# A fused attention and feed-forward kernel: the fold of a pair's exponentials moves to GpSimd, and later input loads are issued by ScalarE

## The chip, the core and the metric

The kernel runs on one core of a Trainium2 chip. The metric is the device time of one execution in microseconds. Engines are named as in the profile: PE is TensorE (PEld its weight loads), DVE is VectorE, ACT is ScalarE, POOL is GpSimd, SP is SyncE. A queue name with q (SPq, ACTq) stands for DMA issues and semaphore waits of that engine's instruction stream.

## The reference

Two stages in fp32. Attention has 4 batches, 8 heads, 768 positions and head size 64; a query sees the 96 positions up to its own, and the first 8 positions of the sequence. Its result, reshaped to 3072 x 512, goes through a two-layer network of width 2048.

```
scores = scale * (q @ k^T);  keep = is_global | is_local
scores = where(keep, scores - slope[h] * dist, -1e9)
a = exp(scores - max); a = a / (sum(a) + 1e-9)
attn_out = a @ v
h = x @ w_in;  g = h * sigmoid(h);  out = g @ w_out
```

## The kernel before

**Tiling.** The sequence of each batch is cut into 6 blocks of 128 queries, 24 blocks in all (i = 0 to 23, j = i mod 6). A block has four pairs of heads. For one pair the scores are 232 columns: 96 keys of the preceding block, 8 global keys, 128 own keys. Two blocks make a group of 256 rows for the network, 12 groups in all. fp32 values are split into a high and a low fp32r part, and products are formed from three matmuls (high by high, high by low, low by high).

**One block of attention.** `load` (L513) fetches keys, queries and values of block i (tiles kn, qn, vn; line L520). `turn` (L557) transposes keys and queries on PE (L560). From block 6 on, ACT and DVE build split and stacked copies (L602, L600, L604, L619, L613). `stack_scores` (L628) forms the scores of one pair. On DVE `top_of` (L680) adds the bias and takes the maximum; on ACT `expo` (L688) takes the exponential with its sum; DVE forms the inverse (L695, L699); ACT scales (L708).

**The folded blocks.** The 15 blocks with i >= 7 and j > 0 are folded. Their 96 preceding keys are 96 of the 128 rows of the block before, and for each query a preceding key is seen only where the own key of the same row is not. So `fold` (L713 to L716) adds the 96 preceding exponentials onto the last 96 own ones, in place, in tile pe. `collect` (L721) copies the 8 global columns to FARS. `turn_folded` (L736, and L739 for the globals of two pairs) transposes the sum on PE, `part_p` (L744) separates it into the two parts by a mask, `move_far` (L751) brings in the globals, and `values` (L789) multiplies by vn and by vp, the preceding values. There are 60 pairs in folded blocks.

**The network.** `pair_h` (L1079) forms two 128-wide pieces of the hidden layer, 24 matmuls of 256 columns. ACT takes tanh (L1085), DVE forms the gate (L1091), POOL forms four sums and differences (L1097), ACT rounds to the high part gh (L1121), DVE forms the low part gl (L1127), and `pair_o` (L1156) multiplies by the second weights with 21 matmuls, some of them from tiles tx and ty, which are loaded from a scratch in HBM for every group (L1065, L1069). At a group's end DVE adds up the results (L1188), and L1024 stores them. Between these, DVE also reads the weights and the values for a range check (L473, L490).

**What sets the order.** `Plan` is a planner in the kernel's own Python code. Every operation is entered by `op(engine, cost, rank, emit, deps, uses, lat)`; `run` (L104) plays the machine forward with these costs and latencies, at each moment gives a free engine the ready operation of the lowest rank, and so fixes the order in which the instructions of each engine stand. SP's DMA issues are one more planner engine, "DMA". The engines then run their streams in that order and wait on semaphores. Buffers are counted there too: kn and qn take two of twelve slots of the shared tag m, vn has two slots.

**Places that the change touches.** The load itself, L520; the planner entries of the loads of k and q (L846) and of v (L879); `fold`, L716, and its planner entry, L923. The blocks from NJ + NB = 8 on are the ones whose loads of k and q wait in the plan for the preceding transposition (`before["t"]`).

Of the kernel before, what the change touches and what calls it, by code (L numbers as in the profile page):

```python
# [17 lines left out]
ALU = mybir.AluOpType  # L18
# [4 lines left out]
NPREV = 96  # L23
# [163 lines left out]
def attn_moe(ctx, tc, q, k, v, n_global, n_local, w_in, w_out, out):  # L187
    nc = tc.nc
# [4 lines left out]
    NJ = S // P  # L193
    NCC = DM // P
    NFC = DFF // P
    NB = 2
# [166 lines left out]
    op = plan.op  # L363
    FIRST = -1e6
    DVE = lambda n: 1000 * (62 + n) / 960
    ACT = lambda n, over=61: 1000 * (over + n) / 1200
# [86 lines left out]
    for n in range(2 * NFC):  # L453
        rank = PAR["C0"] + PAR["CR"] * n
        a, m, x = [] if lent(n) is not None else [Buf("big")], Buf("mid", "m"), lent(n)
        o = op("DMA", 1456, rank - PAR["LW"], (lambda n=n: stage(n, "w")), [o_l[x]] if not a else (), a, PAR["DW"])
# [56 lines left out]
    def load(i, nm, h0=0, h1=H):  # L513
        b, j = divmod(i, NJ)
        pool, tag = (sb2, "vn") if nm == "v" else (sb3, in_kind(i, nm))
        pool = mid if tag == "m" else pool
        if not h0:
            blk[i][nm] = pool.tile([P, H, D], F32, name=f"{nm}n", tag=tag, bufs=dict(vn=2, m=NM2, big=4)[tag])
        src = dict(k=k, q=q, v=v)[nm]
        nc.sync.dma_start(  # L520
            blk[i][nm][:, h0:h1], src[b, h0:h1, j * P:(j + 1) * P, :].rearrange("h p d -> p h d")
        )

# [189 lines left out]
    def fold(i, hp):  # L713
        x = blk[i]["p", hp]
        o = x[:, :, C1 + NGAP:]
        nc.vector.tensor_add(o, o, x[:, :, :NPREV])  # L716

    def collect(i, hp):
        t = blk[i]
# [106 lines left out]
    before, held, joint = {}, [], None  # L826
    for i in range(B * NJ):
# [15 lines left out]
        for nm in "kq" if i else "":  # L843
            xn, tp = Buf("big") if in_kind(i, nm) == "big" else Buf("qkn", "m"), Buf("tq")
            hi, lo = kk[nm.upper() + "H"], kk[nm.upper() + "L"]
            o = op("DMA", 1456, rank - lr if i < NJ + NB else FIRST + rank, (lambda i=i, nm=nm: load(i, nm)), () if i < NJ + NB else [before["t"]], [xn], PAR["DL" if i < NJ else "DX"])  # L846
            stacked = i >= PAR["I0"]
            own = [] if nm == "q" or not stacked or not j else [
                op("POOL", cost, rank, (lambda i=i, x=x, gl=gl: carry(i, x, gl)), [before["s"]], [kk["KH"], kk["KL"]])
# [21 lines left out]
        if j and i < PAR["I0"]:  # L871
            old = o_k[i - 1]
            for gl, cost in ((True, 270), (False, 540)):
# [2 lines left out]
                    [*(old[z] for z in ([("kh", *x) for x in PARTS] if i == 1 else ("kh",))), old.get(("KH", True)), ob["kh"]],  # L876
                    [kb[i - 1]["KH"], kk["KH"]],
                )
        o_v = [op("DMA", 1456, rank - lr + 1, (lambda i=i: load(i, "v")), (), [kk["vn"]], PAR["DL" if i < NJ else "DX"])]  # L879
        arrived = o_v[0]  # L880
        if j:
            o_v.append(op("DMA", 1456 if folded(i) else 750, rank - lr + 1, (lambda i=i: load_prev(i)), o_vg if folded(i) else before["v"],
# [5 lines left out]
        for hp in range(NHP):  # L888
# [31 lines left out]
            o = op("DVE", 72, u - PAR["RI"], (lambda i=i, hp=hp: inverse(i, hp)), [o], [pe])  # L920
            if folded(i):
                far = [op("ACT", 480, u - PAR["RN"], (lambda i=i, hp=hp, a=a: norm(i, hp, a)), [o], [pe]) for a in range(2)]
                o = [op("DVE", 360, u - PAR["RN"], (lambda i=i, hp=hp: fold(i, hp)), far, [pe])]  # L923
                fb = before["far"] if hp % 2 else Buf("far")
                before["far"] = fb
                o.append(op("POOL", 300, u - PAR["RN"], (lambda i=i, hp=hp: collect(i, hp)), far, [pe, fb]))
                deps = [*o, joint]
                if not hp % 2:
                    deps = [o[0], joint]
                    before["collect"] = o[-1]  # L930
                else:
                    deps.append(before["collect"])
                o = op("PE", 328 if hp % 2 else 219, u - PAR["RP"], (lambda i=i, hp=hp, tp=tp: turn_folded(i, hp, tp)), deps, [pe, tp, *([fb] if hp % 2 else [])])
                o_m.append(op("DVE", 690, u - PAR["RM"], (lambda i=i, hp=hp: part_p(i, hp)), [o, before.get("move"), o_keep], [tp, pt]))
                before["move"] = o_m[-1]
                if hp % 2:
                    o_m.append(op("ACT", 550, u - PAR["RM"], (lambda i=i, hp=hp: move_far(i, hp)), o_m[-2:], [tp, pt, pts[-1]]))
                pts.append(pt)
                continue
# [681 lines left out]
```

## Time and profile before

| | |
|---|---|
| median of 3 runs | 665.17 us (664.48 to 665.78) |
| the profiled execution | 665.22 us, its span 663.5 us |
| PE busy | 652.3 us, 98% of the span |
| DVE busy | 570.9 us, 86% |
| ACT busy | 463.1 us, 70% |
| POOL busy | 173.8 us, 26% |
| granted TensorE clock | 1.00 in every stretch read |
| DMA engines | 74.4% of the span by SP's queue, 212 GB/s of HBM traffic |

The span runs from the first instruction to the last; the execution's time is 1.7 us longer. A busy share is an average over stages. Matmuls overlap, so that a busy PE says only that no gap was seen between one matmul's modelled end and the next one's start; the pace of the matmuls shows in the distance of their starts, or in the length of a run of them in the chain of work that ended last.

### The profile page before, as it was taken

Reading aid. Unit: us, or ns where it says so; the run is one execution under the profiler, and the core shown is the slowest. Engines: PE = TensorE matmul, PEld = TensorE weight load, DVE = VectorE, ACT = ScalarE, POOL = GpSimd, SP = SyncE. Lnnn points to the kernel's source line nnn. Section 1 sums busy time; section 2 is a strip of 40 time slices with the busy share of each in tenths; the row PEclk is TensorE's granted clock in tenths of the full one; section 3 lists DMA queues with packets and bytes.
Section 4 is the critical chain, followed back from the end, with each engine's and each line's share of the span. In section 5 each row is a group of like instructions: output and inputs, shape, how many; then the busy total and the mean of one; then the engine's idle time right before and its main releaser. Section 6 shows DMA issues by size and latency. Waiting matters only on the chain.

```text
span 663.5 us, 15861 instructions
## 1 busy us (share of the span) xinstructions
PE 652.3 (98%) x5666; PEld 624.6 (94%) x5666; DVE 570.9 (86%) x1554; ACT 463.1 (70%) x1146; POOL 173.8 (26%) x403
## 2 busy tenths in 40 slices
PE   7999999999999999999999999999999999999997
PEld 5788999889999999999999999999999999999997
DVE  7999999988878889978888988997897987996745
ACT  6997544588677777865877877785677787683333
POOL 3100000000104424424333434243343342442331
PEclk9999999999999999999999999999999999999999
DMA  9998857576798699759679668668867776868742
GB/s 183 234 295 243 245 172 234 165 238 194 215 270 231 195 274 263 229 167 279 196 202 251 190 191 230 208 205 221 257 194 195 236 228 181 261 165 206 218 157 82
DMA packets 157437, 142.62 MB, mean 215 GB/s; under 512 B 100228, under 2 KB 128324, under 8 KB 157356
## 3 DMA queue, kind: packets, MB, share of 16 engines
q1 hardware_dynamic: 157352, 141.58, 74.4%
q8 instruction: 45, 0.74, 0.5%
q14 instruction: 36, 0.29, 0.1%
q10 hardware_dynamic: 4, 0.00, 0.0%
HBM read 121.42 MB, written 19.12 MB: 212 GB/s over the span
## 4 chain that ended last, share of the span: by engine, by line
PE 91%; DVE 5%; ACT 2%; DMA 1%; issue 1%; ACTq 0%; DVEq 0%
PE bank L1079 34%; PE bank L1156 29%; PE bank L976 6%; PE bank L1001 6%; PE bank L789 5%; PE bank L628 5%; PE bank L560 2%; PE bank L736 2%; PE bank L764 1%; DVE pe L680 1%; DVE pe L710 1%; ACT pe L688 1%; DMA ts<-raww 1%; PE bank L739 0%; PE bank L1434 0%
## 5 line engine op out<-in xcount | busy, mean ns | idle before, releaser
L1097 POOL TENSOR_TENSOR sg<-sg 128x128 f32<-128x128 f32 x279 | 131.4, 491 | 217.6 <-DVE sg L1091 165.1
L1079 PE MATMUL bank<-xh,WIH 128*128 128x256 f32 x640 | 182.9, 286 | 0.0
L1079 PE MATMUL bank<-xl,WIH 128*128 128x256 f32 x640 | 178.0, 278 | 0.0
L1079 PE MATMUL bank<-xh,WIL 128*128 128x256 f32 x640 | 177.9, 278 | 0.0
L1127 DVE TENSOR_TENSOR gl<-sg,gh 128x512 fp32r<-128x512 f32 (+1 forms) x152 | 99.1, 653 | 28.5 <-ACT gh L1121 23.8
L1079 PEld LDWEIGHTS bank<-xh,WIH 128*128 128x128 f32 x640 | 120.6, 188 | 1.7 <-issue 1.2
L1121 ACT CAST gh<-sg 128x512 fp32r<-128x512 f32 (+1 forms) x152 | 84.6, 567 | 53.9 <-PE bank L1156 37.0
L1079 PEld LDWEIGHTS bank<-xl,WIH 128*128 128x128 f32 x640 | 120.6, 188 | 0.7 <-DVE xl L810 0.3
L1079 PEld LDWEIGHTS bank<-xh,WIL 128*128 128x128 f32 x640 | 120.4, 188 | 0.0
L688 ACT ACTIVATE pe<-pe,NM 128x232 f32<-128x232 f32 (+1 forms) x192 | 90.0, 472 | 13.1 <-DVE NM L680 11.1
L1085 ACT ACTIVATE sg<-bank 128x512 f32<-128x512 f32 x80 | 47.7, 596 | 42.1 <-PE bank L1079 41.1
L680 DVE CUSTOM_DVE_ANT_0 pe<-bank,B 128x232 f32<-128x232 f32 (+1 forms) x192 | 66.5, 373 | 8.1 <-PE bank L628 7.1
L1156 PE MATMUL bank<-WOH,gh 128*128 128x256 f32 (+1 forms) x280 | 73.3, 292 | 0.0
L1156 PE MATMUL bank<-WOL,gh 128*128 128x256 f32 (+1 forms) x280 | 72.6, 290 | 0.0
L708 ACT ACTIVATE pe<-pe,sm 128x232 f32<-128x232 f32 x132 | 58.6, 482 | 14.4 <-DVE sm L699 13.8
L1091 DVE SCALAR_TENSOR_TENSOR sg<-sg,bank 128x512 f32<-128x512 f32 x80 | 54.7, 684 | 12.9 <-ACT sg L1085 12.2
L1156 PEld LDWEIGHTS bank<-WOH,gh 128*128 128x128 f32 x280 | 52.8, 188 | 0.9
L1156 PEld LDWEIGHTS bank<-WOL,gh 128*128 128x128 f32 x280 | 52.7, 188 | 0.9
L1156 PE MATMUL bank<-WOH,gl 128*128 128x256 f32 (+1 forms) x280 | 49.5, 292 | 0.0
L1156 PE MATMUL bank<-tx,gh 128*128 128x256 f32 x288 | 46.9, 281 | 0.0
L721 POOL COPY FARS<-pe 128x16 f32<-128x16 f32 x60 | 17.5, 298 | 110.7 <-ACT pe L708 108.3
L744 DVE TENSOR_TENSOR pt<-bank,KEEP 128x512 f32<-128x512 f32 x60 | 41.0, 686 | 6.2 <-PE bank L739 4.2
(177 smaller groups left out, 1622.1 us busy)
## 6 DMA issues: line engine op xcount, KB each, us to landing
tx<-ts SPq DMA_DIRECT2D x72, 512.0 KB, 4.3
ty<-ts SPq DMA_DIRECT2D x72, 256.0 KB, 4.6
c<-in_moe_w_in_dram SPq DMA_DIRECT2D x16, 512.0 KB, 5.2
c<-in_moe_w_out_dram SPq DMA_DIRECT2D x16, 512.0 KB, 5.0
vn<-in_v_dram SPq DMA_DIRECT2D x24, 256.0 KB, 5.1
w<-in_moe_w_in_dram SPq DMA_DIRECT2D x12, 512.0 KB, 4.9
w<-in_moe_w_out_dram SPq DMA_DIRECT2D x12, 512.0 KB, 4.8
kn<-in_k_dram SPq DMA_DIRECT2D x23, 256.0 KB, 4.5
```

What stands on the lines that cost most here:

```text
L680: nc.vector.tensor_tensor_reduce(t["p", hp][:, a, :n], t["s", hp][a][:, :n], B1[:, hp] if i % NJ else B0[:, hp], -SC / (1 + a), 3.0e38, AL ...
L688: nc.scalar.activation(x, x, AF.Exp, bias=max_of(i, h), scale=-1.0, accum_out=t["sum", hp][:, a:a + 1],)
L708: nc.scalar.mul(x, x, t["inv", hp][:, a:a + 1])
L744: nc.vector.tensor_tensor(x, t["tp", hp].unsqueeze(1).to_broadcast([P, 2, 2, P]), KEEP.unsqueeze(2).to_broadcast([P, 2, 2, P]), ALU.mult)
L976: nc.tensor.matmul(ph, w[:, c, fs], x[:, c], start=not c and not n, stop=c == NCC - 1 and n == 2)
L1079: nc.tensor.matmul(ph[:, a], w[:, cc, fs], x[:, cc], start=not cc and not m, stop=cc == NCC - 1 and m == 2)
L1085: nc.scalar.activation(x[:, 0:4].rearrange("p (a b) c -> p a (b c)", a=2), mo["ph", g, n], AF.Tanh, scale=0.5)
L1091: nc.vector.scalar_tensor_tensor(x, x, 1.0, mo["ph", g, n], ALU.add, ALU.mult)
L1097: (eng.tensor_sub if e else eng.tensor_add)(x[:, o], x[:, a], x[:, b])
L1121: nc.scalar.copy(mo["gh", g, n][:, a:b], mo["sg", g, n][:, a + o:b + o])
L1127: nc.vector.tensor_sub(mo["gl", g, n][:, a:b], mo["sg", g, n][:, a + o:b + o], mo["gh", g, n][:, a:b].bitcast(F32))
L1156: nc.tensor.matmul(o, l, r, start=(g, b) not in opened, stop=n == NFC // 2 - 1 and m == 2 and (p in ((2, 7, 5, 3, 4) if g == NGRP - 1 else ...
```

## The change

1. `fold` is done by GpSimd (`nc.gpsimd.tensor_tensor(..., ALU.add)`) and not by VectorE. Its planner entry is ("POOL", 600) in place of ("DVE", 360).
2. The loads of keys, queries and values of blocks 8 to 23, 16 blocks with 3 loads each, are issued by ScalarE (`nc.scalar.dma_start`) and not by SyncE. Their planner entries take ACT for 420 in place of the DMA issue engine for 1456, and their latency is raised by 1000. The load of v now has a dependence on the preceding transposition too.

```diff
-        nc.sync.dma_start(
+        (nc.scalar if i >= NJ + NB else nc.sync).dma_start(
             blk[i][nm][:, h0:h1], src[b, h0:h1, j * P:(j + 1) * P, :].rearrange("h p d -> p h d")
         )
...
         o = x[:, :, C1 + NGAP:]
-        nc.vector.tensor_add(o, o, x[:, :, :NPREV])
+        nc.gpsimd.tensor_tensor(o, o, x[:, :, :NPREV], ALU.add)
...
-            o = op("DMA", 1456, rank - lr if i < NJ + NB else FIRST + rank, (lambda i=i, nm=nm: load(i, nm)), () if i < NJ + NB else [before["t"]], [xn], PAR["DL" if i < NJ else "DX"])
+            o = op(*(("DMA", 1456) if i < NJ + NB else ("ACT", 420)), rank - lr if i < NJ + NB else FIRST + rank, (lambda i=i, nm=nm: load(i, nm)), () if i < NJ + NB else [before["t"]], [xn], PAR["DL"] if i < NJ else PAR["DX"] + 1000 * (i >= NJ + NB))
...
-        o_v = [op("DMA", 1456, rank - lr + 1, (lambda i=i: load(i, "v")), (), [kk["vn"]], PAR["DL" if i < NJ else "DX"])]
+        o_v = [op(*(("DMA", 1456) if i < NJ + NB else ("ACT", 420)), rank - lr + 1, (lambda i=i: load(i, "v")), () if i < NJ + NB else [before["t"]], [kk["vn"]], PAR["DL"] if i < NJ else PAR["DX"] + 1000 * (i >= NJ + NB))]
...
-                o = [op("DVE", 360, u - PAR["RN"], (lambda i=i, hp=hp: fold(i, hp)), far, [pe])]
+                o = [op("POOL", 600, u - PAR["RN"], (lambda i=i, hp=hp: fold(i, hp)), far, [pe])]
```

Since the planner's costs change, the order moves on every engine from the ninth block on; the number of matmuls does not change. Three places follow, before and after.

VectorE at the end of the seventh group of the network, order before (ost is the group's result, few the range check's tile, sm the sums of one pair):

```order
L1091 SCALAR_TENSOR_TENSOR sg<-sg,bank_113 128x512
L744 TENSOR_TENSOR pt<-bank_115,KEEP 128x512
L695 TENSOR_SCALAR sm<-sm 128x2
L490 TENSOR_REDUCE few<-vn 128x1
L1188 SCALAR_TENSOR_TENSOR ost<-bank_119,ost 128x256
L1188 SCALAR_TENSOR_TENSOR ost<-bank_114,ost 128x256 x3
L1188 SCALAR_TENSOR_TENSOR ost<-bank_117,ost 128x256 x2
L1188 SCALAR_TENSOR_TENSOR ost<-bank_120,ost 128x256
L1127 TENSOR_TENSOR gl<-sg,gh 128x384
L699 RECIPROCAL sm<-sm 128x2
L613 SCALAR_TENSOR_TENSOR KH<-bank_116,KH 64x4x128
L1127 TENSOR_TENSOR gl<-sg,gh 128x512
```

The same place on VectorE, order of the change:

```order
L1091 SCALAR_TENSOR_TENSOR sg<-sg,bank_114 128x512
L744 TENSOR_TENSOR pt<-bank_117,KEEP 128x512
L1188 SCALAR_TENSOR_TENSOR ost<-bank_119,ost 128x256
L1188 SCALAR_TENSOR_TENSOR ost<-bank_120,ost 128x256 x3
L1188 SCALAR_TENSOR_TENSOR ost<-bank_113,ost 128x256 x2
L1188 SCALAR_TENSOR_TENSOR ost<-bank_115,ost 128x256
L1127 TENSOR_TENSOR gl<-sg,gh 128x384
L695 TENSOR_SCALAR sm<-sm 128x2
L613 SCALAR_TENSOR_TENSOR KH<-bank_118,KH 64x4x128
L1127 TENSOR_TENSOR gl<-sg,gh 128x512
```

Between the gate (L1091) and the second low part (the last row) the range check L490 and one of the two small steps on sm are gone and stand elsewhere. At the tenth group's end, which has the same rows before, the check stays where it was and only the step on sm goes.

GpSimd in the twelfth block, order before:

```order
L1097 TENSOR_TENSOR sg<-sg 128x128 x8
L721 COPY FARS<-pe 128x16 x3
L1097 TENSOR_TENSOR sg<-sg 128x128 x4
L721 COPY FARS<-pe 128x16
L1097 TENSOR_TENSOR sg<-sg 128x128 x12
```

The same block on GpSimd, order of the change:

```order
L1097 TENSOR_TENSOR sg<-sg 128x128 x8
L716 TENSOR_TENSOR pe<-pe 128x2x96
L721 COPY FARS<-pe 128x16
L716 TENSOR_TENSOR pe<-pe 128x2x96
L721 COPY FARS<-pe 128x16
L716 TENSOR_TENSOR pe<-pe 128x2x96
L1097 TENSOR_TENSOR sg<-sg 128x128 x4
L721 COPY FARS<-pe 128x16
L1097 TENSOR_TENSOR sg<-sg 128x128 x4
L716 TENSOR_TENSOR pe<-pe 128x2x96
L721 COPY FARS<-pe 128x16
L1097 TENSOR_TENSOR sg<-sg 128x128 x8
```

Every fold now stands in GpSimd's stream among the network's sums: 32 of the 60 come directly behind a set of them, and a set can stand between a fold and its collect.

ScalarE in the third batch, around the loads of block 13 (queries and values) and block 14 (keys), order before:

```order
L688 ACTIVATE pe,sm<-pe,NM 128x128
L1121 CAST gh<-sg 128x384
L602 CAST KH<-bank_114 64x4x128
L602 CAST KL<-bank_114 64x4x128
L1121 CAST gh<-sg 128x512
L1085 ACTIVATE sg<-bank_116 128x512
L1121 CAST gh<-sg 128x384
L602 CAST QH<-bank_119 64x512
L1121 CAST gh<-sg 128x512
L600 ACTIVATE QL<-bank_119 64x512
```

The same place on ScalarE, order of the change:

```order
L688 ACTIVATE pe,sm<-pe,NM 128x128
L1121 CAST gh<-sg 128x384
L520 DMA qn<-in_q_dram 128x8x64
L602 CAST KH<-bank_119 64x4x128
L1121 CAST gh<-sg 128x512
L602 CAST KL<-bank_119 64x4x128
L1085 ACTIVATE sg<-bank_118 128x512
L1121 CAST gh<-sg 128x384
L520 DMA kn<-in_k_dram 128x8x64
L1121 CAST gh<-sg 128x512
L520 DMA vn<-in_v_dram 128x8x64
L602 CAST QH<-bank_117 64x512
```

The three issues of a block stand between casts of the network's high parts and casts of the stacked keys and queries; the load of queries stands just ahead of the casts of the keys that were transposed before it.

## Rows read from the trace of the kernel before

**Rows 1.** Page, part 1: busy us, share of the span, instructions.

```profile
PE 652.3 (98%) x5666; PEld 624.6 (94%) x5666; DVE 570.9 (86%) x1554; ACT 463.1 (70%) x1146; POOL 173.8 (26%) x403
```

**Rows 2.** Stretches: length, busy PE, PEld, DVE, ACT, POOL; clock, DMA, GB/s.

```profile
200.00:250.00 50.00, 50.00 (x456) 49.09 (x455) 44.37 (x109) 38.35 (x93) 19.87 (x43) 1.00 0.76 228
...
640.00:663.50 23.50, 19.72 (x174) 19.52 (x173) 13.23 (x28) 7.20 (x14) 4.47 (x8) 1.00 0.21 65
```

**Rows 3.** Waits of PE, then of PEld, 160 to 600 us: total, times, longest.

```profile
PE bank L1156 <- DVE gl L1127: 0.6, 2, 0.3
...
PEld bank L1156 <- DVE gl L1127: 1.0, 2, 0.5
```

**Rows 4.** Timeline of PE, 417 to 418.5 us.

```profile
417.90 0.28 PE L1156 MATMUL bank<-WOH,gl 128*128 128x256 f32 x1
418.47 0.38 PE L1156 MATMUL bank<-tx,gl 128*128 128x256 f32 x1 [0.29 <-DVE gl L1127]
```

**Rows 5.** Chain that ended last: start, length; runs of 24 matmuls of 256 columns.

```profile
203.16 2.83 PE bank L1079 x24
...
611.11 2.72 PE bank L1079 x24
```

**Rows 6.** Timeline of DVE, 410 to 419 us: start, length, what.

```profile
413.12 0.67 DVE L490 TENSOR_REDUCE few<-vn 128x1 f32<-128x512 f32 x1
413.71 2.73 DVE L1188 SCALAR_TENSOR_TENSOR ost<-bank,ost 128x256 f32<-128x256 f32 x7
...
417.01 0.68 DVE L613 SCALAR_TENSOR_TENSOR KH<-bank,KH 64x512 fp32r<-64x512 f32 x1
417.72 0.69 DVE L1127 TENSOR_TENSOR gl<-sg,gh 128x512 fp32r<-128x512 f32 x1
```

**Rows 7.** Line L716, the fold: ns min/median/max, first and last start.

```profile
L716 DVE TENSOR_TENSOR pe<-pe x60: 341/358/639, 164.3 to 600.3; 128x192 f32<-128x192 f32 x60
```

**Rows 8.** Adds of two SBUF tiles: line L1097, then POOL's groups.

```profile
L1097 POOL TENSOR_TENSOR sg<-sg x279: 449/462/843, 201.3 to 654.1; 128x128 f32<-128x128 f32 x140
L1097 DVE TENSOR_TENSOR sg<-sg x9: 291/293/552, 646.2 to 655.4; 128x128 f32<-128x128 f32 x9
...
L1193 POOL TENSOR_TENSOR ost<-ost 128x256 f32<-128x256 f32 x1 | 0.7, 737 | 3.9 <-ACT ost L1185 3.9
```

**Rows 9.** Two folds and the transpositions that read them: timelines of DVE and PE.

```profile
418.93 0.35 DVE L716 TENSOR_TENSOR pe<-pe 128x192 f32<-128x192 f32 x1
...
419.52 0.27 PE L736 MATMUL bank<-ident,pe 128*128 128x128 f32 x1
...
443.92 0.35 DVE L716 TENSOR_TENSOR pe<-pe 128x192 f32<-128x192 f32 x1
...
445.34 0.27 PE L736 MATMUL bank<-ident,pe 128*128 128x128 f32 x1
```

**Rows 10.** Issues of DMAs, lines L520 and L267; landing of L520's, 160 to 640.

```profile
L520 SPq DMA_DIRECT2D qn<-in_q_dram x25: 380/385/1072, 1.4 to 569.4; - x25
...
L267 ACTq DMA_DIRECT2D raw<-in_n_global_dram x1: 511/511/511, 1.1 to 1.1; - x1
...
DMA to landing us min/median/max: 3.5/5.0/7.1
```

**Rows 11.** Waits on SP's queue, 160 to 600 us, of the loads for a buffer.

```profile
SPq L520 <- PE bank L789: 8.8, 4, 3.7
SPq L520 <- PE bank L736: 8.4, 6, 2.3
```

**Rows 12.** One load of queries on SP and the transposition that reads it.

```profile
333.08 0.38 SPq L520 DMA_DIRECT2D qn<-in_q_dram  x1
...
339.27 0.27 PE L560 MATMUL bank<-ident,qn 128*128 128x128 f32 x1
```

**Rows 13.** Page, part 5: one of three like groups of L1079.

```profile
L1079 PE MATMUL bank<-xh,WIH 128*128 128x256 f32 x640 | 182.9, 286 | 0.0
```

## The prediction

> **What bounds the kernel.** I read the page's busy shares first: TensorE is busy 98% of the span, VectorE 86%, ScalarE 70%, GpSimd 26% [rows 1]. Shares do not say whether TensorE waits, so I went to the stretches. From 200 to 250 us, where attention and network run side by side, TensorE is busy 50.00 of 50 us, VectorE 44.4, ScalarE 38.4, GpSimd 19.9; its only long gap lies at the very end, 23.5 - 19.7 = 3.8 us, which the last results and stores take [rows 2]. Then the waits, in the part that the change can reach: from 160 to 600 us matmuls waited 0.6 us in two pieces and weight loads 1.0 us in two pieces, all for a low part gl from VectorE [rows 3]. One of these places in full: the matmul on tx starts 0.57 us after its predecessor, where 0.11 is due, so 0.45 us are lost [rows 4, 5]; VectorE had been busy without a gap and delivered that gl only at 418.4, behind a range check of 0.67 us, seven result additions of 2.73 us, and a key step of 0.68 us [rows 6]. So TensorE is the bound, and all that better cover can give back after 160 us is 2 x 0.45 = 0.9 us. The number of matmuls stays. A measurement of this kernel can tell about 0.2% from no change, 1.33 us: this change cannot reach that on the fast side by removing waits, but it can on the slow side by making new ones.
>
> **The fold leaves VectorE.** 60 additions of 0.36 us at the median [rows 7] are 21 us of VectorE's 571. By itself that gives nothing: VectorE's time lies beside TensorE's. It counts only where VectorE is late, in the two gl waits. In the new order of the seventh group's end the range check no longer stands ahead of the result additions, and the gl comes at least 0.6 us earlier against 0.45 us lost: -0.45 us. At the tenth group's end the check stays and only a short step on sm goes, so I take half: -0.2 us. Bounds for both: 0, if something else of VectorE falls in there, and -1.0 us, the whole of the weight loads' waits [rows 3].
>
> **The fold comes to GpSimd.** Its price there is not in the trace. GpSimd's add of 128 columns takes 462 ns at the median, its one add of 256 takes 737 ns [rows 8]; on the line between them 192 columns cost about 0.60 us. The lower bound is 0.46 (the 128-column add), the upper 0.98 (0.60 plus the 0.38 by which the slowest 128-column add exceeds the median one). I take 0.60, since both ends of the line are the same operation. 60 of them are 36 us, and GpSimd rises from 174 to 210 us of 663: it is not a bound. What counts is the latency of one pair, since its transpositions wait for it: +0.24 us, and up to 4 x 0.46 = 1.84 us more where the fold waits through a whole set of the network's sums; 32 of the 60 folds stand directly behind a set.
>
> The room for it: in the kernel before a fold ends 0.24 us before its transpositions start at one of the tightest places (419.28 to 419.52) and 1.07 us at a usual one (444.27 to 445.34) [rows 9]. The order gives more: from a pair's last score matmul to its transpositions TensorE now has on the mean eleven more 256-column matmuls of other work over the 60 pairs, at 2.72 / 24 = 0.113 us each [rows 5] 1.3 us. So at a usual place 1.07 + 1.3 = 2.4 us of room stand against at most 0.24 + 1.84 = 2.1 us of new latency. I cost it at 0.2 us, a few tight places; bounds 0 and the rival below. The cover is other matmuls; where it is gone, TensorE stands for the difference.
>
> **The loads go to ScalarE.** 48 issues leave SyncE. One took 0.385 us there at the median, the larger of the two issues seen on ScalarE 0.511 [rows 10]: 18 to 25 us more on ScalarE, spread over some 400 us, about 2 to 3 us in a stretch of 50 in which it has 11.6 us idle [rows 2]. Cost on the path: 0, covered by that idle time. Behind a waiting issue now stand ScalarE's tanh, casts and exponentials. On SyncE these loads waited 8.8 us in four pieces for the values' matmuls (vn) and 8.4 us in six for a pair's transpositions, 2.3 at most [rows 11]. The wait for the values costs ScalarE little, because the casts of the attention result that follow it wait for the same matmuls; only the issue's 0.4 us is added, beside TensorE's next group of matmuls. A wait of a key or query load would stop ScalarE, but ScalarE reaches the issue in its own order, in the rows of the change next to casts that read TensorE's results of the same moment, where SyncE came early and had nothing else to do. I take 0; bounds 0 and 8.4 us, if every one of those waits went through to TensorE.
>
> The landing must also be in time. A query load on SyncE was issued 6.2 us before its transposition, one of the shortest distances [rows 12], and the loads land after 5.0 us at the median, 7.1 at most [rows 10]. In the new order the issue still stands by the casts of the keys transposed just before, so I take the same distance and 0.
>
> **Sum.** 665.22 (profiled execution) - 0.45 - 0.2 + 0.2 + 0 = **664.8 us**; the median of the runs shown, 665.17, is the same within 0.05.
>
> **Rivals.**
> *Nothing goes away.* The order is new on every engine; new small waits of the same kind as the two of now make up for them. For it: eight group ends, each with seven additions in a row on VectorE. Against it: VectorE has 21 us less to do. 665.2 us, no change.
>
> *Folds come late.* On GpSimd, an in-order stream, a fold stretched to 0.98 us behind a full set of sums ends 0.62 + 1.84 = 2.46 us later than now; the room at a usual place is 2.37. At tight places (0.24 + 1.3 = 1.54) TensorE stands for up to 0.92 us. If 8 of the 32 are tight this is 7.4 us, about 672; if two or three are, 2 to 3 us, about 667. It decides at a fold of about 0.9 us. For it: the spread of GpSimd's add, 449 to 843 ns [rows 8]. Against it: the median is near the minimum. The Trainium skill ("GPSIMD Engine Reference", Specifications) says that GpSimd shares its SBUF interfaces with VectorE and contends with VectorE instructions that read two SBUF inputs; by that rule the fold meets the gl subtractions, which read two, and the 843 ns fits it, though no row here shows which instruction ran beside. The same page (section 4.1) puts two-input elementwise work on GpSimd at about twice VectorE's time; the same 128-column add here takes 462 against 293 ns, 1.6 times [rows 8], so the trace agrees in direction with less. This rival ends slower.
>
> *Query loads come late.* If ScalarE reaches the issue 2 us later than SyncE did, a landing of 5.0 us misses the transposition by 5.0 + 2 - 6.2 = 0.8 us; 16 query loads make 12.8 us, 677 us; only the shortest six, 670. For it: ScalarE is busy three quarters of the time there. Against it: the plan puts a raised latency on these loads, and the casts beside the issue must run early too. The Trainium skill ("DMA: Bandwidth & Descriptors", Issuing engines are not separate DMA queues) says that DMAs from all issuers share the same 16 DMA engines and that issuing from several saves only issue time; by it landings stay at about 5 us and no load arrives sooner. No run here shows it yet.
>
> *The pace of matmuls shifts.* Runs of 24 like matmuls take 2.72 us in some places and 2.83 in others [rows 5], with nothing waited for. Of the 1920 of this line (three groups of 640) [rows 13] each tenth that changes pace is 192 x 4.6 ns = 0.9 us. A fifth of them at the faster pace would give 664.8 - 1.8 = 663.0; as many at the slower one 666.6. I see no reason for either sign.
>
> **Chances.** The forecast 0.55; nothing goes away 0.18; folds late 0.11; query loads late 0.05; pace faster 0.06, slower 0.05. Faster than 663.84: the pace and a bit of the forecast, 0.08. Slower than 666.5: folds and loads late and a part of the pace, 0.17. The rest, 0.75, is no change. For eight in ten I leave out most of the late loads, the worse half of the late folds and the far end of the faster pace: 663.8 to 667.2.
>
> **What would show it.** Right: TensorE's wait for gl at the seventh group's end gone and that at the tenth's shorter, L716 on GpSimd at about 600 ns, no wait of the transpositions L736 for GpSimd over 0.3 us, no wait of L560 for qn, VectorE's busy time down by about 25 us and ScalarE's queue with 48 issues of about 0.4 us. Wrong: TensorE waiting for pe from GpSimd at many pairs, a fold near 1 us, or an L520 on ScalarE that waits over a microsecond with tanh behind it and gh late.

## The result, and the profile after

| | before | after |
|---|---|---|
| median | 665.13 us (664.48 to 665.78) | 670.64 us (669.99 to 671.88) |
| profiled execution, its span | 665.22, 663.5 us | 671.88, 670.2 us |
| first to last matmul of the profile | 1.44 to 659.44 us | 1.45 to 663.94 us |
| last matmul to the end of the span | 4.05 us | 6.23 us |

The ratio is 1.0083, with a 95% interval of 1.0071 to 1.0095: 5.5 us slower, where 664.8 and a range up to 667.2 were forecast. Here and below, executions over 1.5% longer than the fastest of their kernel are left out of the ratios, though not of the medians. The profiled execution lost 6.7 us; 4.5 lie between the first and the last matmul, 2.2 behind the last one.

The page of the changed kernel answers to [rows 1]: VectorE lost 18 us, GpSimd gained 35. In the shares of the chain of waits (its third line here) a DMA of queries now has 4%; that counts the whole flight of loads, not what was lost.

```profile
PE 657.0 (98%) x5666; PEld 628.7 (94%) x5666; DVE 552.7 (82%) x1494; ACT 463.1 (69%) x1146; POOL 208.9 (31%) x463
...
PE 86%; DVE 5%; DMA 5%; ACT 2%; issue 1%; POOL 0%; SPq 0%; ACTq 0%
PE bank L1079 32%; PE bank L1156 27%; PE bank L976 6%; PE bank L1001 6%; PE bank L789 5%; PE bank L628 4%; DMA qn<-in_q_dram 4%; PE bank L560 2%; PE bank L736 2%; DVE pe L680 1%; PE bank L764 1%; DVE pe L710 1%; DVE xl L810 1%; ACT pe L688 1%; DMA ts<-raww 1%
```

**Waits.** The same view as [rows 3], after. The two waits for gl are gone, and new ones stand there: three for query loads, one for xl, the low part of the attention result.

```profile
PE bank L560 <- DMA qn<-in_q_dram: 1.1, 3, 0.7
PE bank L1079 <- DVE xl L810: 0.4, 1, 0.4
```

One of the three in full, from the timelines of ScalarE and of TensorE. The load is issued at 518.84, and the transposition that reads it starts 7.7 us later, 1.01 us behind its predecessor where 0.11 is due. The same distance at the other two places gives 0.34 and 0.40 us lost, 1.6 in all; at xl 0.5 are lost.

```profile
518.84 0.38 ACTq L520 DMA_DIRECT2D qn<-in_q_dram  x1
```

```profile
525.55 0.28 PE L1079 MATMUL bank<-xh,WIL 128*128 128x256 f32 x1
526.56 0.41 PE L560 MATMUL bank<-ident,qn 128*128 128x128 f32 x2 [0.73 <-DMA qn<-in_q_dram]
```

**The fold and the issues.** Lines L716 and L520 of the changed kernel, against [rows 7] and [rows 10], and the landing of the query loads from 160 to 640 us. The fold takes 598 ns at the median, an issue on ScalarE 374. No row has TensorE waiting for a fold: by the timelines a fold ends at least 0.41 us ahead of its transpositions and 1.57 at the median, where these were 0.20 and 0.95 before.

```profile
L716 POOL TENSOR_TENSOR pe<-pe x60: 589/598/1044, 164.4 to 605.1; 128x192 f32<-128x192 f32 x60
```

```profile
L520 ACTq DMA_DIRECT2D qn<-in_q_dram x16: 374/374/407, 172.1 to 573.6; - x16
...
DMA to landing us min/median/max: 3.4/5.1/7.6
```

A fold and the subtraction that forms gl on VectorE hold each other up where they meet, and it is the later one that pays. In 22 of their 36 meetings (of over 0.1 us) the fold starts first and takes 598 ns at the median; in 14 it starts second and takes 912. A subtraction of 512 columns takes 686 ns where GpSimd does nothing and 1075 beside a fold (for over 0.3 us), one of 384 columns 548 and 834. One meeting with the fold first, from the timelines of GpSimd and VectorE:

```profile
329.85 0.59 POOL L716 TENSOR_TENSOR pe<-pe 128x192 f32<-128x192 f32 x1
```

```profile
329.89 1.10 DVE L1127 TENSOR_TENSOR gl<-sg,gh 128x512 fp32r<-128x512 f32 x1
```

In all, the subtractions cost VectorE 5 us more. Their line in the page before, and after:

```profile
L1127 DVE TENSOR_TENSOR gl<-sg,gh 128x512 fp32r<-128x512 f32 (+1 forms) x152 | 99.1, 653 | 28.5 <-ACT gh L1121 23.8
```

```profile
L1127 DVE TENSOR_TENSOR gl<-sg,gh 128x512 fp32r<-128x512 f32 (+1 forms) x152 | 104.0, 685 | 38.2 <-ACT gh L1121 37.2
```

**The pace.** TensorE is busy without a gap in the last stretch of both kernels, at a granted clock of 1.00, but starts 310 matmuls in 35 us before and 300 after. First the stretch of the kernel before, then that of the changed one (columns as in [rows 2]), then the chain of the changed kernel: its runs of 24 take 2.83 us where those of before take 2.72 [rows 5].

```profile
620.00:655.00 35.00, 35.00 (x310) 34.84 (x309) 21.55 (x51) 12.64 (x23) 10.77 (x23) 1.00 0.49 154
```

```profile
625.00:660.00 35.00, 35.00 (x300) 35.00 (x299) 18.51 (x35) 12.23 (x22) 9.13 (x20) 1.00 0.47 151
```

```profile
635.25 2.83 PE bank L1079 x24
...
640.55 2.83 PE bank L1079 x24
```

I counted the distances from start to start of all neighbouring matmuls of 256 columns from 150 us on. There are two clusters, around 113.3 and 117.8 ns (I take 116 as the border). Of some 3250, 1167 are slow before and 1690 after: 523 x 4.5 ns = 2.4 us (about a hundred of the slow ones, in every kernel, are the longer first distances behind an insertion). The pace does not change at random: it is taken within some five matmuls behind an insertion (transpositions, scores, values), and mostly stays until the next one. In the last stretch before, 441 in a row are fast but for a few behind each insertion; after, 409 in a row are slow.

**The end.** TensorE's row of the branch at L1447, which leads past the general arm: before, then after. SyncE waits for TensorE there, and the span ends 2.2 us later.

```profile
L1447 PEldq COMPARE_BRANCH  x1: 385/385/385, 661.1 to 661.1; - x1
```

```profile
L1447 PEldq COMPARE_BRANCH  x1: 3597/3597/3597, 665.5 to 665.5; - x1
```

The other end of this: TensorE's stream has 134 semaphore instructions of its own where it had 85, most of the 49 new ones at the transpositions of the folded pairs. The same line before and after:

```profile
L736 PEldq EVENT_SEMAPHORE  x1: 51/51/51, 247.5 to 247.5; - x1
```

```profile
L736 PEldq EVENT_SEMAPHORE  x30: 51/51/51, 225.3 to 594.9; - x30
```

**The sum of the profiled execution:** end 2.2, pace 2.4, queries 1.6, xl 0.5, gl -0.9, which is 5.8 of the 6.7. The remaining 0.9 lie ahead of the change: the network's first matmul comes at 142.4 us and not at 141.4 in an order that is still the same, and in the experiments this offset ran from -0.2 to 0.7. Three kernels with the same order up to the last stretch (queries on SyncE, two and four spare transpositions, below) have 0.0 to 0.1 there, so I put it down to the execution, which is the longest of the four, and not to the change.

### The profile page after: what moved, and what is told of

It reads as the page before. It is cut to its first block, busy times and chain, and to the rows that moved or that the text cites. A ratio compares the mean times of both kernels' runs of the same rounds, so it can differ in the third digit from the quotient of the medians.

```text
span 670.2 us, 15913 instructions
## 1 busy us (share of the span) xinstructions
PE 657.0 (98%) x5666; PEld 628.7 (94%) x5666; DVE 552.7 (82%) x1494; ACT 463.1 (69%) x1146; POOL 208.9 (31%) x463
## 4 chain that ended last, share of the span: by engine, by line
PE 86%; DVE 5%; DMA 5%; ACT 2%; issue 1%; POOL 0%; SPq 0%; ACTq 0%
PE bank L1079 32%; PE bank L1156 27%; PE bank L976 6%; PE bank L1001 6%; PE bank L789 5%; PE bank L628 4%; DMA qn<-in_q_dram 4%; PE bank L560 2%; PE bank L736 2%; DVE pe L680 1%; PE bank L764 1%; DVE pe L710 1%; DVE xl L810 1%; ACT pe L688 1%; DMA ts<-raww 1%
## 5 line engine op out<-in xcount | busy, mean ns | idle before, releaser
L1097 POOL TENSOR_TENSOR sg<-sg 128x128 f32<-128x128 f32 x279 | 127.0, 476 | 224.2 <-DVE sg L1091 133.4
L1079 PE MATMUL bank<-xh,WIH 128*128 128x256 f32 x640 | 182.9, 286 | 0.0
L1079 PE MATMUL bank<-xl,WIH 128*128 128x256 f32 x640 | 178.3, 279 | 0.4 <-DVE xl L810 0.4
L1079 PE MATMUL bank<-xh,WIL 128*128 128x256 f32 x640 | 178.2, 278 | 0.0
L1127 DVE TENSOR_TENSOR gl<-sg,gh 128x512 fp32r<-128x512 f32 (+1 forms) x152 | 104.0, 685 | 38.2 <-ACT gh L1121 37.2
L1079 PEld LDWEIGHTS bank<-xh,WIH 128*128 128x128 f32 x640 | 120.9, 189 | 1.9 <-issue 1.4
L1079 PEld LDWEIGHTS bank<-xl,WIH 128*128 128x128 f32 x640 | 120.5, 188 | 1.3 <-DVE xl L810 0.9
L1079 PEld LDWEIGHTS bank<-xh,WIL 128*128 128x128 f32 x640 | 120.4, 188 | 0.0
L1091 DVE SCALAR_TENSOR_TENSOR sg<-sg,bank 128x512 f32<-128x512 f32 x80 | 54.6, 683 | 24.7 <-ACT sg L1085 23.9
L1156 PE MATMUL bank<-WOH,gh 128*128 128x256 f32 (+1 forms) x280 | 74.1, 294 | 0.0
L1156 PE MATMUL bank<-WOL,gh 128*128 128x256 f32 (+1 forms) x280 | 73.2, 291 | 0.0
L716 POOL TENSOR_TENSOR pe<-pe 128x192 f32<-128x192 f32 x60 | 40.2, 669 | 83.9 <-ACT pe L708 83.4
L1156 PEld LDWEIGHTS bank<-WOH,gh 128*128 128x128 f32 x280 | 52.9, 189 | 0.9
L1156 PEld LDWEIGHTS bank<-WOL,gh 128*128 128x128 f32 x280 | 52.8, 189 | 0.9
L744 DVE TENSOR_TENSOR pt<-bank,KEEP 128x512 f32<-128x512 f32 x60 | 41.3, 688 | 10.7 <-PE bank L736 7.0
L1156 PE MATMUL bank<-WOH,gl 128*128 128x256 f32 (+1 forms) x280 | 49.7, 292 | 0.0
L1156 PE MATMUL bank<-tx,gh 128*128 128x256 f32 x288 | 48.0, 285 | 0.0
```

Of the source, the lines that this page charges most:

```text
L744: nc.vector.tensor_tensor(x, t["tp", hp].unsqueeze(1).to_broadcast([P, 2, 2, P]), KEEP.unsqueeze(2).to_broadcast([P, 2, 2, P]), ALU.mult)
L1079: nc.tensor.matmul(ph[:, a], w[:, cc, fs], x[:, cc], start=not cc and not m, stop=cc == NCC - 1 and m == 2)
L1091: nc.vector.scalar_tensor_tensor(x, x, 1.0, mo["ph", g, n], ALU.add, ALU.mult)
L1097: (eng.tensor_sub if e else eng.tensor_add)(x[:, o], x[:, a], x[:, b])
L1127: nc.vector.tensor_sub(mo["gl", g, n][:, a:b], mo["sg", g, n][:, a + o:b + o], mo["gh", g, n][:, a:b].bitcast(F32))
L1156: nc.tensor.matmul(o, l, r, start=(g, b) not in opened, stop=n == NFC // 2 - 1 and m == 2 and (p in ((2, 7, 5, 3, 4) if g == NGRP - 1 else ...
```

## The experiments

All ratios are against runs of the kernel before on the same chip. The table gathers what the texts need: the 256-column matmuls at the slow pace, the time that TensorE lost to late query loads (by the distances of starts ahead of L560), how many more instructions its stream has than before, and its branch. Where only the profile shows a thing, it is that of one execution.

| kernel | median us, ratio | slow matmuls | lost to qn, us | more instr. | branch us |
|---|---|---|---|---|---|
| before | 665.13 | 1167 | 0 | 0 | 0.39 |
| after | 670.64, 1.0083 | 1690 | 1.6 | 49 | 3.60 |
| fold alone | 665.84, 1.0007 (0.9998 to 1.0015) | 1561 | 0 | 34 | 0.38 |
| loads alone | 666.71, 1.0026 (1.0003 to 1.0050) | 1244 | 1.9 | 17 | 0.38 |
| new order, old engines | 669.49, 1.0059 (1.0045 to 1.0073) | 1681 | 0 | 34 | 0.39 |
| old order, new engines | 672.20, 1.0084 (1.0063 to 1.0104) | 1077 | see text | 49 | 3.66 |
| after, 4 spare | 669.10, 1.0063 (1.0049 to 1.0076) | 1334 | 0.7 | 57 | 0.48 |
| before, 2 spare | 665.19, 1.0002 (0.9993 to 1.0011) | 1095 | 0 | 4 | 0.39 |
| fold, 4 spare | 667.35, 1.0035 (1.0022 to 1.0049) | 1103 | 0 | 42 | 3.58 |
| before, longer stream | 667.16, 1.0034 (1.0023 to 1.0046) | 1120 | 0 | 56 | 3.88 |
| fold, 4 spare, shorter stream | 664.67, 0.9980 (0.9971 to 0.9990) | 1129 | 0 | 28 | 0.39 |
| after, queries on SyncE | 669.60, 1.0059 (1.0046 to 1.0072) | 1740 | 0 | 49 | 3.84 |
| after, shorter stream | 667.42, 1.0023 (1.0011 to 1.0035) | 1717 | 0.3 | 33 | 0.39 |
| after, 2 spare | 669.58, 1.0067 (1.0049 to 1.0085) | 1335 | 0.8 | 53 | 3.66 |
| four for two at L736 | 674.05 (one run) | 1652 | 0.2 | 169 | 0.38 |
| three for two at L736 | 670.02 (one run) | 1499 | 0 | 109 | 0.38 |

**Fold alone.** Of the change only the fold's two lines:

```diff
-        nc.vector.tensor_add(o, o, x[:, :, :NPREV])
+        nc.gpsimd.tensor_tensor(o, o, x[:, :, :NPREV], ALU.add)
...
-                o = [op("DVE", 360, ...)]
+                o = [op("POOL", 600, ...)]
```

> Fold on GpSimd with its planner entry of 600, all loads left on SyncE with their old entries. My theory (the loss of 5.5 us is made of query loads that land late, of long runs of 256-column matmuls that fall on the slow pace of 118 ns instead of 113, and of a branch at the very end that takes TensorE 3.6 us): no wait of L560 for qn; the wait for gl stays away or shrinks; the pace may fall either way, since the order is a new one (plus or minus 2.4 us), so 664 to 667.5 us. Rival (GpSimd's adds take SBUF time from TensorE, so that its matmuls slow down): share of matmuls at 118 ns up to about a half as in the changed kernel, 667 to 669 us, also without the loads.

No wait for gl and none for the fold, as forecast, 0.9 us back; but 394 matmuls more at the slow pace, 1.8 us. By these two it would be 0.9 us slower; 0.6 were measured, and the interval does not tell that from nothing. The rival's slow share of a half did come, without its price of 667 to 669; whether GpSimd makes it, the third run tells.

**Loads alone.** The other three lines of the change.

> 48 loads issued by ScalarE with their new planner entries, the fold left on VectorE. My theory: TensorE waits for qn at L560 in some two to five places, 1 to 2 us in all, plus what the new order does to the pace (plus or minus 2.4 us): 665.5 to 669 us. Rival (the fold on GpSimd is what slows the matmuls): share of slow matmuls as before, about a third, and 665 to 667 us.

One query load came late and cost 1.9 us, and one matmul stood 0.9 us for a tile tx, which SyncE loads. The waits for gl are gone here too, with the fold still on VectorE, and the pace is nearly as before. Its runs reach from 664.37 to 673.99 us, where those of the fold alone stay within 665.56 to 666.51. Loads that land just in time or just late would scatter the time like this; only one of these runs has a profile, so that is not shown.

**The order without the engines, and the engines without the order.** The first is the changed kernel with the two emitted lines put back, its three planner entries kept; the second is the kernel before with the two emitted lines of the change and its own planner entries.

```diff
-        (nc.scalar if i >= NJ + NB else nc.sync).dma_start(
+        nc.sync.dma_start(
...
-        nc.gpsimd.tensor_tensor(o, o, x[:, :, :NPREV], ALU.add)
+        nc.vector.tensor_add(o, o, x[:, :, :NPREV])
```

> The planner entries of the change, so its order of instructions on TensorE, VectorE, ScalarE and GpSimd, but the fold is emitted on VectorE and the loads on SyncE. If the order sets the pace: the matmuls fall on the same paces as in the changed kernel, the last stretch at 118 ns, slow share about a half, 667 to 669 us, no wait for qn. If the engines set it (GpSimd's adds, ScalarE's queue): slow share back to a third, last stretch at 113 ns, 664.5 to 666 us.

> The planner entries of the kernel before, so its order, but the fold is emitted on GpSimd and the 48 loads on ScalarE at the places where SyncE had them. If the order sets the pace: slow share about a third as before, last stretch at 113 ns; what is added are the loads, which now stand where ScalarE meets them early or late, 665 to 668 us. If the engines set it: slow share about a half and 668 to 671 us.

The new order alone, with the old engines, has a ratio of 1.0059 of the 1.0083. The pace goes with the order, and not with GpSimd or ScalarE's queue: 1681 slow matmuls in the new order without any of the new engines, 1077 in the old order with all of them. The last stretch of the new order with the old engines, in the chain:

```profile
634.27 2.83 PE bank L1079 x24
...
639.58 2.83 PE bank L1079 x24
```

And of the old order with the new engines:

```profile
622.13 2.72 PE bank L1079 x24
...
642.86 2.72 PE bank L1079 x24
```

The wait for xl is in the first of the two as well (0.4 us by the same row), so it belongs to the order too. In the second, issued from ScalarE at places meant for SyncE, the query loads cost far more: 6.5 us of waits of matmuls in five places in its profiled execution. That one took 678.67 us where the other six took 668.39 to 673.47, so that the size for the others is not shown. Behind the two longest of these waits its granted clock was 0.5 (1.2 GHz) for 3.4 us each, and 1.00 (2.4 GHz) otherwise from 10 us to the last matmul; that can add to the 1077 slow matmuls, not take from them.

The waits for gl follow the order as well as the fold. In the old order with the new engines both stand, although VectorE has no folds to do; in the new order with the old engines two others of 0.37 us each by the starts stand at other places:

```profile
PE bank L1156 <- DVE gl L1127: 0.6, 2, 0.3
```

```profile
PE bank L1156 <- DVE gl L1127: 0.4, 2, 0.2
```

Both kernels took longer than I expected of the order: 669.49 us against 667 to 669, and 672.20 against 665 to 668, above the other theory's 671 as well; neither the long branch nor query waits of this size were priced there. One thing does not add up: the new order with the old engines has a short branch and no wait for queries in its profile (668.93 us, the second shortest of its six runs), yet the same ratio as the changed kernel with its queries back on SyncE (last below), whose branch is long. What its other runs spend is open.

**Four spare transpositions in the changed kernel.** Behind the last matmuls of the values, at the start of the last stretch:

```diff
+    def spare(last, tp):
+        x = lambda: [nc.tensor.transpose(bank(tp, NHP, P)[:, m], ident, ident) for m in range(4)]
+        op("PE", 10, -2, x, [last], [tp])
...
-            joint = last
+            joint = last; i == B * NJ - 1 and spare(last, Buf("tp"))
```

> The changed kernel with four spare transpositions of the identity (the form of L560's) behind the last matmuls of the values, and no other instruction moved. Theory (what is inserted before a run of 256-column matmuls sets its pace, and it stays until the next insertion; behind four transpositions of L560's form 22 of 27 runs of the changed kernel are fast): the 409 matmuls of the last stretch go from 118 to 113 ns, 409 x 4.45 ns = 1.8 us less, against 0.44 us for the transpositions: 1.4 us faster than the changed kernel, about 669.2 us beside 670.6, so 1.006 of the kernel before. Rival (the last stretch is slow because of what else the changed kernel does, or the pace is chance): it stays at 118 ns and the kernel is 0.4 us slower than the changed one.

The same edit with two in the kernel before, with four on the fold alone, and with two in the changed kernel:

> The kernel before with two spare transpositions (the form of L736's) behind the last matmuls of the values, and no other instruction moved. Theory (behind two transpositions 20 of 21 runs of the kernel before are slow): its last stretch of 441 matmuls goes from 113 to 118 ns, 441 x 4.45 ns = 2.0 us, with 0.22 us for the transpositions 2.2 us slower, 667.4 us, ratio 1.003. Rival: it stays fast, 665.4 us.

> Only the fold moved, with four spare transpositions behind the last matmuls of the values. Theory: the last stretch of 412 matmuls, slow with the fold alone, becomes fast: 1.8 us less, 0.44 us more, so 1.4 us under the 665.8 of the fold alone, 664.4 us, ratio 0.999, a little under the kernel before, with no wait for gl and none for qn. Rival: the last stretch stays slow, 666.3 us.

> The changed kernel with two spare transpositions (not four) behind the last matmuls of the values. If any insertion of transpositions there ends the slow pace, the last stretch is fast: 1.8 us less, 0.2 more, 669 us. If it takes four, the last stretch stays at 118 ns: 670.8 us. In the kernel before two of them left the fast pace as it was, against what I expected.

Four made the slow last stretch fast, in the changed kernel and on the fold alone; so did two in the changed kernel. In the two edits of the changed kernel one short step on VectorE changed places with its neighbour as well; on the fold alone nothing else moved. In the changed kernel with four, the chain reads:

```profile
613.19 0.59 PE bank L582 x4
...
633.16 2.72 PE bank L1079 x24
```

So what stands just ahead of a long stretch can turn its pace, which is not tied to the rest of the change. But my rule "two make it slow" fell: in the kernel before two of them left the stretch fast. Nor did the time of the fold with four follow: its last matmul starts at 658.42 us, 1.0 before that of the kernel before, and yet it is 2.3 us slower, because the branch now took 3.58 us. The changed kernel with four has a branch of 0.48 us in its profile of 666.51 us, its other four runs took 668.59 to 669.80; whether their branch was long is not shown.

**Number or place.** At the even pairs two spare transpositions, then one, behind L736's two, 30 times:

```diff
-        for a in range(2):
-            nc.tensor.transpose(ps[:, a], t["p", hp][:, a, C1:], ident)
+        for a in range(2 if hp % 2 else 4):
+            nc.tensor.transpose(x[:, a * P:(a + 1) * P], t["p", hp][:, a, C1:] if a < 2 else ident, ident)
```

> The changed kernel with two spare transpositions of the identity behind the two of every even pair (L736), so that four of one form stand in a row, 30 times, order otherwise the same. If the number in a row sets the pace (behind four at L560 22 of 27 runs are fast, behind two at L736 17 of 19 slow in the changed kernel): at most a quarter of the runs behind these four are slow, some 400 matmuls fewer at the slow pace, -1.8 us, against 30 x 0.22 = 6.6 us of transpositions: 675 us. If it is something else of the place (what TensorE waits for or what it reads), they stay slow: 677 us.

> The same with one spare transposition, so three in a row. If the number sets it, a share of slow runs between that of two and that of four, near the half of the odd pairs, which have three (12 of 25 slow). If something else sets it, slow as before. 30 x 0.11 = 3.3 us more, 673 to 674 us.

Of the 19 stretches of matmuls that stand behind these alone, 17 went at 118 ns with two, 6 with three, 7 with four. The insertion thus matters, but not by a count: behind the odd pairs, where nothing was added, the stretches at 118 ns went from 12 of 25 to 20 with four and 11 with three at the even ones, so a place also depends on what came before it. What picks the pace is open. The times, one execution each, lie under what I expected (674.05 us against 675 to 677, 670.02 against 673 to 674): in both the branch came out short, which I had not foreseen.

**A longer and a shorter stream.** In the kernel before, each of the 14 warm-up matmuls at the very start becomes three; in two other kernels 7 or 6 of double width take the place of the 14 (`calls` counts the calls, and every second emits nothing):

```diff
-        nc.tensor.matmul(bank(b, 2 * P), warm[:, :P], warm, start=True, stop=True)
+        [nc.tensor.matmul(bank(b)[:, c:d], warm[:, :P], warm[:, c:d], start=True, stop=True) for c, d in ((0, P), (P, 192), (192, 2 * P))]
```

```diff
-        nc.tensor.matmul(bank(b, 2 * P), warm[:, :P], warm, start=True, stop=True)
+        len(calls) % 2 or len(calls) > 11 or nc.tensor.matmul(bank(b), warm[:, :P], warm, start=True, stop=True); calls.append(b)
```

> The kernel before with each of the 14 warm-up matmuls at its start cut into three of together the same columns: 56 more instructions on TensorE's stream, nothing else moved. Theory (the length of TensorE's stream decides whether the target of the branch at L1447 is there or has to be fetched first: the branch took 0.38 us with 85, 102 and 119 extra semaphore instructions and 3.6 us with 134): the branch takes about 3.6 us, and the kernel ends 2 to 3 us later, 667 to 668.5 us, ratio 1.003 to 1.005, with the same paces and waits as before. Rival (the long branch comes of the new engines, for instance of ScalarE's DMA queue): it stays at 0.38 us, 665.3 us.

> The changed kernel with 16 instructions fewer on TensorE (6 warm-up matmuls of 512 columns in place of 14 of 256), so 33 over the kernel before in place of 49. Theory: the branch takes 0.4 us and not 3.6, all else as in the changed kernel: 2.2 us less, about 668.4 us, ratio 1.005. Rival: the branch is long for another reason of the change and stays so, 670.6 us.

> The fold alone on GpSimd, four spare transpositions behind the last values, and 14 instructions fewer on TensorE: its 14 warm-up matmuls of 256 columns become 7 of 512. Theory (length of the stream decides over the branch; with the 8 instructions of the spare transpositions it stood 42 over the kernel before and took 3.58 us, now 28 over, which is less than the 34 over at which the fold alone took 0.38): branch 0.4 us, the body as with the spare transpositions (last matmul at 658.4 us), so 2.4 us under that run, 664.2 to 664.9 us, 0.9985 to 0.9995 of the kernel before. Rival (the branch's time is chance): it stays long, 667 us.

56 instructions more, and nothing else, give the kernel before the long branch and 2.1 us:

```profile
L1447 PEldq COMPARE_BRANCH  x1: 3878/3878/3878, 660.7 to 660.7; - x1
```

16 fewer take it from the changed kernel, 3.2 us in all (2.2 expected), of which its profile shows 1.3 as shorter waits for queries. Over all sixteen profiles the branch is short up to 34 instructions more, long from 42 to 56, and short again at 57, 109 and 169. So it is a matter of where the stream ends, and the traces show a fetch in this place. A queue that they mark as instruction, q8, brings pieces of 16 KB: 45 in the seven profiles with up to 34 instructions more, 46 in the nine from 42 on, so that its count follows TensorE's stream. In all six with the long branch a piece starts while the branch stands, 0.7 to 1.5 us into it (in the changed kernel at 666.55 us, the branch lasting from 665.52 to 669.12). In the ten with the short one none does; at 57, 109 and 169 the additional piece has started 2.9 to 10.7 us ahead of the branch. First the page before, then after:

```profile
q8 instruction: 45, 0.74, 0.5%
```

```profile
q8 instruction: 46, 0.75, 0.5%
```

The Trainium skill ("Runtime: NRT & Kernel Launch", Instruction fetch mechanics) says that a taken branch whose target lies outside the two pages held has to wait for that page; by that rule the cost comes and goes with the length, and the trace agrees. At 57 the piece comes the least ahead, and the four other runs of that kernel are 2.1 to 3.3 us longer than its profiled one; whether a length so near the border falls either way is not shown.

The last kernel, fold alone with four spare transpositions and the shorter stream, is the best: 664.67 us (664.40 to 665.11). In this measurement the runs of the kernel before scattered from 664.8 to 667.5, which flatters its ratio of 0.998; against their medians of 665.0 to 665.3 elsewhere it is 0.9991 to 0.9995, less than can be told.

**Queries back on SyncE.** The changed kernel, order and all else the same:

```diff
-        (nc.scalar if i >= NJ + NB else nc.sync).dma_start(
+        (nc.scalar if i >= NJ + NB and nm != "q" else nc.sync).dma_start(
```

> The changed kernel with the query loads of blocks 8 to 23 alone back on SyncE, at the same places of the plan; keys and values stay on ScalarE, and the order of the other engines is the same. Theory (query loads that ScalarE issues late and that wait there behind its work cost 1.6 us in the profile): no wait of L560 for qn over 0.3 us, the pace as in the changed kernel, 669 us or, where the shorter stream also shortens the branch, 667; runs closer together. Rival (the raised latency of the plan, not the engine, puts these loads late): the waits for qn stay, 670 us.

The waits for qn are gone, and the runs lie within 0.5 us (669.39 to 669.89) where those of the changed kernel span 1.9. The same load as above, from the timelines of SyncE and TensorE: issued at 517.12, 7.48 us ahead of its transposition, which starts without a gap.

```profile
517.12 0.43 SPq L520 DMA_DIRECT2D qn<-in_q_dram  x1
```

```profile
524.48 0.28 PE L1079 MATMUL bank<-xh,WIL 128*128 128x256 f32 x1
524.60 0.60 PE L560 MATMUL bank<-ident,qn 128*128 128x128 f32 x4
```

Of the eleven query loads from 300 us on, SyncE's issue stands 7.5 us or more ahead of the transposition in this order, ScalarE's 5.8 to 7.7. The landings take up to 6.7 us here and 7.6 in the changed kernel. So what made them late is the engine that issues them, not the plan's raised latency.

## Why the prediction was wrong, point by point

The terms that the sum had were nearly right. What failed is what it put at 0 or left out: the pace of the matmuls (2.4 us of the profiled execution), the branch behind the last matmul (2.2), the landing of the queries (1.6) and a wait for xl (0.5).

- **gl waits, -0.65 us:** they went as forecast, small in size: both whole, -0.9 us, also at the tenth group's end, where I took half. The reason is the order more than the lighter VectorE: with the fold on GpSimd in the old order both stayed, and with the loads alone they went while the fold was still on VectorE.
- **The fold's price, 0.60 us:** right, 598 ns; the line between the adds of 128 and 256 columns held. The Trainium skill's factor of about two ("GPSIMD Engine Reference", section 4.1) is 598 / 358 = 1.67 here [rows 7]. Its slowest was 1044 ns, beyond my upper bound of 0.98. The rival had no row for what runs beside a slow add: it is the gl subtractions, and they pay too, 104.0 us in all where they took 99.1, a part of why VectorE's busy time fell by 18 us and not by the 25 that I listed as a sign.
- **The fold's latency, +0.2 us, and the rival of late folds:** no wait came, so 0 and not 0.2; 14 of the 60 folds took over 0.75 us, and still the cover of other matmuls held in the changed kernel and with the fold alone. In the old order, without the eleven matmuls more, none came either.
- **Issues on ScalarE, 0:** right, 374 ns each at the median (one load of values 986), and no wait of more than 0.22 us ahead of one. SyncE's long waits for a buffer [rows 11] did not move to ScalarE.
- **Landing, "I take the same distance and 0":** wrong. ScalarE reached the issues later than SyncE had. For the eleven query loads from 300 us on the distance was 6.2 to 8.9 us before, 8.4 at the median, and is 5.8 to 7.7 now, 7.2 at the median and with the waits counted in. Landings of up to 7.6 did not fit: +1.6 us in the profile, less in that of the shorter stream. This is the rival of late query loads, sized there at 12.8 us for a delay of 2 us at all sixteen. Landings stayed at 5.1 us at the median, 5.3 before; the Trainium skill's rule that another issuing engine saves only issue time ("DMA: Bandwidth & Descriptors", Issuing engines are not separate DMA queues) agrees.
- **The pace:** wrong. I saw the two paces and wrote "no reason for either sign" with a chance of 0.11 for both together. A new order draws the pace of every stretch anew, the longest with it, and 2.4 us came out at the slow one. The rival's arithmetic was right; its chance and its place (only L1079, where L1156 follows the same pace) were not.
- **"The number of matmuls stays":** true, but not enough. The sum has no term for the time behind the last matmul, which I took as given. TensorE's stream is longer by 49 semaphore instructions, and its length decides over 2.2 us at the branch. They are not only the waits for one engine more: the new order with the old engines has 34 of them, the old order with the new engines 49.
- **xl, +0.5 us:** not foreseen; the new order, with either set of engines.

The time fell into the range that I gave the late loads, but by three mechanisms of which they are one; that it fits there is luck.

## What to carry to other kernels

When a plan is re-made, its new order is a change of its own: build it once with the old engines and once the other way round before a gain or a loss is put down to an engine. Moving a load to a busy engine's queue costs little in issue time; what counts is how much later that engine reaches it, against the slowest landing. And count all instructions of a long stream, semaphores too, when the program ends in a branch.

## What the runs showed of the hardware that was not expected

- Matmuls of 256 columns run at 113.3 or at 117.8 ns from start to start, at the same granted clock of 1.00, each for hundreds in a row; the pace is taken behind inserted short matmuls and repeats nearly from kernel to kernel of one order (1690, 1681, 1740 and 1717 matmuls at 118 ns in four kernels of the new order, 1167, 1077 and 1120 in three of the old one).
- A branch on TensorE takes 0.38 to 0.48 us or 3.6 to 3.9 us, by the length of the stream ahead of it: the long ones are those in which a 16 KB piece of the instruction queue q8 starts while the branch stands.
- An add of 192 columns on GpSimd and a subtraction of 512 columns on VectorE, each with two inputs in SBUF, hold each other up when they meet, the later one paying: the add takes 912 ns in place of 598, the subtraction 1075 in place of 686, at the median.
